# Causal mask of a recurrent-memory attention: from mask matmuls to an add on VectorE, with the subtraction of the maximum on GpSimd

## The chip, the cores and the metric

The kernel runs on one core of one Trainium2 chip. The metric is the device time of one execution in microseconds; lower is better. The engines are called PE (TensorE; PEld is its weight load), DVE (VectorE), ACT (ScalarE), POOL (GpSimd) and SP (SyncE, which here issues DMAs).

## The reference

Attention over segments of 32 tokens with 8 memory tokens that are handed from segment to segment, then a feed-forward block. 2048 tokens give 64 segments, which must run one after the other.

```python
S, Dm, H, Dh, M, seg = 2048, 640, 32, 128, 8, 32
idx  = arange(M + seg)
mask = (idx[:, None] < M) | (idx[:, None] >= idx[None, :])
mem  = mem0
for s in range(64):
    h = concat([mem, layernorm(x)[s*32:(s+1)*32]])      # 40 rows
    q, k, v = h @ Wq, h @ Wk, h @ Wv                     # per head
    scores = where(mask, q @ k.T * Dh**-0.5, -1e9)       # 40 x 40 per head
    o = softmax(scores) @ v @ Wo
    mem, out_s = o[:8], o[8:]
h  = x + concat(out_s)
h2 = h + relu(layernorm(h) @ w1 + b1)**2 @ w2 + b2
```

The memory rows of a segment see all 40 keys, the token rows only the keys up to their own.

## The kernel before, in words

The order of the instructions on every engine is the order in which the program issues them (a manual schedule); each engine works through its own list and waits where its data isn't there. One call of `step(b, sp)` handles one segment; 64 of them follow each other, with `b` the block of 128 tokens and `sp` the segment in it. A `tail` of 8 tokens of each segment is projected ahead of time for four segments at once, as work that needs no memory; such work lies in lists (`fill`, `late`, `mid`, `win`), from which `run` takes pieces at fixed places of a step.

Within a step, in this order on PE:

1. `project` (L392) multiplies the 32 rows of the segment (24 tokens and 8 memory rows, `hT4`) with Wq and Wk in halves of 16 heads. ACT takes the result out of PSUM into `row` (L222, L224, L405), DVE transposes it into `qT` and `kT` (L227, L408), POOL spreads the memory queries into `qz` (L374, L376).
2. `scores(n)` (L413) and `soft1`, `soft2` are the scores and the softmax of the memory rows, for `n` = 0 and 1.
3. `token_scores(n)` (L486) are the scores of the tokens of all 32 heads, in one PSUM bank `sk` seen as `skv` [128, 8, 40]: four groups of 32 partitions by eight heads by 40 keys. For `n` = 0 four mask matmuls (L489) stand ahead: the identity times `mask` puts 0 or -1e9 into the columns of the 32 token keys, and the score matmuls (L493) add to that in PSUM.
4. Between these lie the Wv projection (`proj` with `half`, evacuated by ACT in L502 and L523), `token_values` of the step before (L355, L360), and `values(n)` (L449, L454), whose results go to `oT` by DVE (L213) or ACT (L215).
5. DVE takes the maximum of `skv` over the keys (L527, `mxk`) and writes `tk` = `skv` - `mxk` to SBUF (L529).
6. `wo_rounds` (L238) is the output projection of the step's main rows into `pw`, with pieces of `fill` between.
7. ACT takes the exponential of `tk` (L542, `ek`); DVE sums it (L544, `zk`) and inverts the sum (L546, `rk`); POOL multiplies (L548 `pkt`, L551 `pk`).
8. `wo_out` (L241): ACT copies half of `pw` (L245, `otmp`, in the same buffer as `tk`), DVE adds the other half (L246, `o`). `mem_to_hT` (L312) transposes the eight new memory rows on PE (L316, `pm`) and DVE copies them into the next segment's `hT4` (L318). This is the recurrence: the next step's projections can't start before.
9. DVE transposes `pkt` and `pk` (L569 `pTt`, L575 `pTk`) for the `token_values` of the next step.

On ACT the order around the change is L523, L215, L542, L245; on DVE L440, L527, L529, L544, L546, L246, L318, L569, L575; on POOL L374 and L376, then L548, L551, L367 and the copies of the tails (L323, L325).

Of the kernel before, what the change touches and what calls it, by code (L numbers as in the profile page):

```python
# [9 lines left out]
ALU = mybir.AluOpType  # L10
AX = mybir.AxisListType
F32 = mybir.dt.float32
BF16 = mybir.dt.bfloat16
# [3 lines left out]
def kernel(  # L17
# [16 lines left out]
    nc = tc.nc  # L34
    _, S, D = A_x.shape
    _, H, E = A_Wq.shape
    M = A_mem0.shape[1]
    SEG = 32
    G = 4
    HG = H // G  # L40
# [8 lines left out]
    NK = SEG + M  # L49
# [6 lines left out]
    NEG = -1.0e9  # L56
# [4 lines left out]
    const = ctx.enter_context(tc.tile_pool(name="const", bufs=1))  # L61
# [6 lines left out]
    s1 = ctx.enter_context(tc.tile_pool(name="s1", bufs=1))  # L68
# [9 lines left out]
    ident = const.tile([128, 128], BF16)  # L78
# [3 lines left out]
    make_identity(nc, ident[:])  # L82
    mhalf = const.tile([128, 1], F32)
    nc.vector.memset(mhalf[:], -0.5)
    mask = const.tile([128, HG, SEG], BF16)
    nc.vector.memset(mask[:], 0.0)
    nc.gpsimd.affine_select(out=mask[0:32], in_=mask[0:32], compare_op=ALU.is_ge, fill=NEG, base=0,
                            pattern=[[0, HG], [-1, SEG]], channel_multiplier=1)
    bmask = const.tile([128, 4, TL], BF16)
    qz = const.tile([128, H, 32], BF16)  # L90
    nc.vector.memset(qz[:], 0.0)
# [10 lines left out]
    kT = const.tile([128, H, 2 * SEG], BF16)  # L102
# [33 lines left out]
    for ch in range(2):  # L136
        nc.scalar.dma_start(out=o0[32 * ch:32 * ch + M, :].rearrange("m (c f) -> m c f", f=64),
                            in_=A_mem0[0].rearrange("m (c t f) -> t m c f", t=2, f=64)[ch])
# [110 lines left out]
    fill, late, mid, win = [], [], [], []  # L249
# [130 lines left out]
    def step(b, sp, v=None):  # L380
# [53 lines left out]
        def soft2(n):  # L434
            rm = s2.tile([128, 1], F32, tag="rm", name="rm")
            nc.vector.reciprocal(out=rm[:], in_=zms[n][:])
            pm = s2.tile([128, 2 * SEG], BF16, tag="pmem", name="pmem")
            nc.vector.tensor_scalar(out=pm[:], in0=ems[n][:], scalar1=rm[:, 0:1], scalar2=None, op0=ALU.mult)
            pT = s2.tile([128, 2 * SEG], BF16, tag="pTm", name="pTm")
            nc.vector.transpose(out=pT[:], in_=pm[:])  # L440
            return pT
# [42 lines left out]
        skv = sk[:, 0:HG * NK].rearrange("p (i k) -> p i k", k=NK)  # L484

        def token_scores(n):  # L486
            if n == 0:
                for g in range(G):
                    nc.tensor.matmul(skv[32 * g:32 * g + 32, :, M:NK], lhsT=ident[:, 0:32], rhs=mask[:],  # L489
                                     start=True, stop=False, skip_group_check=True)  # L490
            for j in range(4):
                for g in range(G):
                    nc.tensor.matmul(skv[32 * g:32 * g + 32, n * 4 + j, :], lhsT=qT[:, n * 16 + g * 4 + j, M:NK],  # L493
                                     rhs=kT[:, n * 16 + g * 4 + j, 0:NK], start=False, stop=(n == 1 and j == 3),
                                     skip_group_check=True)

        token_scores(0)
        if ready:
            run(fill, DC)
# [8 lines left out]
        if not last:  # L508
            scores(1)
        token_scores(1)  # L510
        if not last:
            soft1(1)
# [10 lines left out]
            nc.scalar.copy(out=v[:, 512:1024], in_=ps1[:])  # L523
        if not last:
            pT1 = soft2(1)
        mxk = s1.tile([128, HG], F32, tag="mxk", name="mxk")
        nc.vector.tensor_reduce(out=mxk[:], in_=skv, op=ALU.max, axis=AX.X)  # L527
        tk = s1.tile([128, HG, NK], F32, tag="tk", name="tk")
        nc.vector.tensor_tensor(out=tk[:], in0=skv, in1=mxk[:].unsqueeze(2).to_broadcast([128, HG, NK]), op=ALU.subtract)  # L529

        pw = chn.tile([128, 512], F32, tag="ch", name="pw")
        main = lambda p: oT[:, p, 0:32]
# [1 line left out]
        if not last:  # L534
# [14 lines left out]
                                op=ALU.mult)  # L549
        pk = s1.tile([128, HG, 32], BF16, tag="pk", name="pk")  # L550
        nc.gpsimd.tensor_tensor(out=pk[:], in0=ek[:, :, 0:SEG], in1=rk[:].unsqueeze(2).to_broadcast([128, HG, SEG]),  # L551
                                op=ALU.mult)
# [18 lines left out]
        for u in range(2):  # L571
            nc.gpsimd.tensor_tensor(out=pTx[:, u], in0=pTt[:, u, HD:32].unsqueeze(1).to_broadcast([128, 4, TL]),
                                    in1=same[:], op=ALU.mult)
# [160 lines left out]
    for b in range(NB):  # L734
        for sp in range(4):
# [47 lines left out]
            if 2 <= e <= NK4 + 1:  # L783
                late.append(lambda e=e: prep_stats0(e - 2))
                mid.append(lambda e=e: prep_norm0(e - 2))
            step(b, sp, v0 if b + sp == 0 else None)

    def end_output(s):
# [18 lines left out]
    for t in range(S // NT):  # L807
# [6 lines left out]
        for fc in range(FC):  # L814
            ps = mmtile()
            for c in range(DC):
                if fc < FFULL:
                    nc.tensor.matmul(ps[:], lhsT=w1[:, c, fc * 128:(fc + 1) * 128], rhs=hnT[:, c, :],  # L818
                                     start=(c == 0), stop=(c == DC - 1))
                    continue  # L820
                for hh in range(2):
                    nc.tensor.matmul(ps[FREM * hh:FREM * (hh + 1), 0:HT], lhsT=w1[:, c, fc * 128:F],
                                     rhs=hnT[:, c, HT * hh:HT * (hh + 1)], start=(c == 0), stop=(c == DC - 1))
# [16 lines left out]
        for q in range(NK4):  # L840
# [6 lines left out]
            for hh in range(2):  # L847
                k = pr + 2 * hh
                for fc in range(FFULL):
                    nc.tensor.matmul(y[:, hh, 0:DH], lhsT=f1T[:, fc, k * 128:(k + 1) * 128], rhs=w2[:, fc, cs],  # L850
                                     start=(fc == 0), stop=False, skip_group_check=True)
# [3 lines left out]
            for hh in range(2):  # L855
                r = slice(FREM * hh, FREM * (hh + 1))
                nc.tensor.matmul(y[:, hh, 0:DH], lhsT=f1T[r, FFULL, pr * 128:(pr + 1) * 128], rhs=w2[r, FFULL, cs],
                                 start=False, stop=True, skip_group_check=True)
# [40 lines left out]
```

## Time and profile before

| | |
|---|---|
| median of 3 runs | 1029.64 us (1028.8 to 1029.67) |
| span of the profiled execution | 1025.5 us |
| the profiled execution's own time | not listed apart; span and median differ by 4.1 us |
| granted PE clock, mean | 0.997 |
| PE busy | 971.4 us (95%) |
| DVE, ACT, POOL busy | 619.0, 533.2, 309.1 us |
| mask matmuls L489 | 256, 273 ns each, 18.4 us |
| score matmuls L493 | 2048, 182 ns each, 36.7 us |
| DVE maximum L527, subtraction L529 | 64 each, 453 and 492 ns |
| ACT exponential L542 | 64, 473 ns |
| POOL products L548, L551 | 64 each, 294 and 615 ns |

Busy times overlap: four matmuls on 32 columns each run side by side, so the durations of the PE groups don't add up to the time that they hold PE. "Idle before" an instruction is the time in which its engine had nothing to do, with what ended it.

### The profile page before, as it was taken

To read this page: it belongs to the slowest core of one execution; us is meant where nothing else is said; L and a number is where in the kernel's file an instruction comes from. 1 tells how busy PE (TensorE), PEld (TensorE's weight loads), DVE (VectorE), ACT (ScalarE), POOL (GpSimd) and SP (SyncE) were. 2 spreads that over 40 slices of the span, in tenths; PEclk is the share of its full clock that TensorE was granted. 3 is DMA by queue.
4 is the path that set the end of the run, shared out by engine and by line. 5 is a ranking of instruction groups with operands and counts; after the bars stand their busy time and mean duration, and the time that the engine had idled before them with its cause. 6 is when DMAs were issued, how large, how long until landed. Compare 5 with 4: busy or idle time off the path is not lost.

```text
span 1025.5 us, 58960 instructions
## 1 busy us (share of the span) xinstructions
PE 971.4 (95%) x26951; PEld 576.6 (56%) x26960; DVE 619.0 (60%) x1740; ACT 533.2 (52%) x1229; POOL 309.1 (30%) x803
## 2 busy tenths in 40 slices
PE   5789999999999999999999999999999999999998
PEld 2345555655655555555655665555566565555565
DVE  2246666766666757666666666666666676466432
ACT  3335554555555555555555555555555555533431
POOL 1123333333333333333333332323232333443210
PEclk9989999999999999999999999999999999999999
DMA  9950101000101010001000000000000110612200
GB/s 367 397 180 21 23 7 30 7 25 6 35 7 31 6 40 8 26 11 31 11 25 11 26 16 20 17 15 27 14 22 8 47 34 7 204 55 65 77 26 26
DMA packets 39112, 51.57 MB, mean 50 GB/s; under 512 B 5968, under 2 KB 35024, under 8 KB 36944
## 3 DMA queue, kind: packets, MB, share of 16 engines
q1 hardware_dynamic: 38080, 47.48, 13.9%
q8 instruction: 210, 3.44, 1.4%
q10 hardware_dynamic: 784, 0.34, 0.1%
q14 instruction: 38, 0.31, 0.1%
HBM read 38.37 MB, written 9.44 MB: 47 GB/s over the span
## 4 chain that ended last, share of the span: by engine, by line
PE 87%; DMA 6%; DVE 2%; issue 2%; ACT 1%; SPq 1%; ACTq 0%; DVEq 0%; POOL 0%; POOLq 0%
PE ps L206 48%; PE pw L238 15%; PE y L850 5%; PE ps L818 4%; PE ps L238 3%; PE po L449 2%; PE po L355 2%; PE sm L421 2%; DMA wq<-in_B_w_dram 1%; DMA vt_d<-row 1%; PE ps L493 1%; DMA wv<-in_A_Wv_dram 1%; DMA wo<-in_A_Wo_dram 1%; PE pm L316 1%; DMA vt<-vt_d 1%
## 5 line engine op out<-in xcount | busy, mean ns | idle before, releaser
L206 PEld LDWEIGHTS <-hT 128*32 128x32 bf16 x7680 | 195.4, 97 | 179.6 <-issue 17.9
L238 PE MATMUL pw<-wo,oT 128*32 128x320 bf16 x4224 | 185.6, 300 | 7.6 <-issue 5.6
L206 PE MATMUL ps<-wv,hT 128*32 128x512 bf16 x2520 | 171.5, 379 | 2.3 <-issue 1.6
L206 PE MATMUL ps<-wq,hT 128*32 128x512 bf16 x2520 | 160.0, 382 | 5.3 <-DVE hT L318 5.3
L206 PE MATMUL ps<-wk,hT 128*32 128x512 bf16 x2520 | 159.3, 381 | 0.1
L238 PEld LDWEIGHTS <-oT 128*32 128x32 bf16 x4224 | 106.7, 96 | 59.8 <-issue 13.0
L222 ACT ACTIVATE row<-ps 128x512 bf16<-128x512 f32 x156 | 93.3, 599 | 75.5 <-PE ps L206 75.5
L227 DVE STREAM_TRANSPOSE qT<-row 128x512 bf16<-128x512 bf16 x128 | 90.3, 705 | 66.0 <-ACT row L222 65.9
L548 POOL TENSOR_TENSOR pkt<-ek,rk 128x64 bf16<-128x64 bf16 x64 | 18.8, 294 | 360.6 <-DVE rk L546 360.6
L224 ACT CAST row<-ps 128x512 bf16<-128x512 f32 x115 | 67.9, 591 | 33.1 <-PE ps L206 31.4
L325 POOL COPY kT<-kTt 128x1024 bf16<-128x1024 bf16 (+1 forms) x65 | 71.8, 1105 | 11.7 <-DVE kTt L227 11.7
L374 POOL COPY qz<-qT 128x96 bf16<-128x96 bf16 x126 | 33.4, 265 | 139.1 <-DVE qT L227 138.9
L206 PEld LDWEIGHTS <-hTt 128*32 128x32 bf16 x1920 | 53.6, 97 | 31.5 <-issue 1.3
L245 ACT COPY otmp<-pw 64x320 f32<-64x320 f32 x66 | 27.9, 422 | 81.3 <-PE pw L238 81.3
L365 ACT CAST oT<-po 128x512 bf16<-128x512 f32 x128 | 68.7, 589 | 1.6
L246 DVE TENSOR_TENSOR o<-pw,otmp 64x320 bf16<-64x320 f32 x66 | 31.8, 482 | 61.3 <-ACT otmp L245 61.3
L523 ACT CAST v<-ps 128x512 bf16<-128x512 f32 x63 | 36.9, 585 | 59.0 <-PE ps L206 59.0
L227 DVE STREAM_TRANSPOSE kT<-row 128x512 bf16<-128x512 bf16 x65 | 46.1, 709 | 31.1 <-ACT row L224 31.1
L544 DVE TENSOR_REDUCE zk<-ek 128x8 f32<-128x320 bf16 x64 | 31.1, 486 | 51.1 <-ACT ek L542 51.1
L850 PE MATMUL y<-wq,wk 128*128 128x320 bf16 x416 | 61.2, 299 | 0.4 <-DVE wk L827 0.4
L405 ACT CAST row<-ps 128x256 bf16<-128x256 f32 x126 | 40.7, 375 | 30.5 <-PE ps L206 29.9
L502 ACT CAST v<-ps 128x512 bf16<-128x512 f32 x63 | 36.9, 585 | 30.5 <-PE ps L206 30.5
(113 smaller groups left out, 1629.5 us busy)
## 6 DMA issues: line engine op xcount, KB each, us to landing
wv<-in_A_Wv_dram SPq DMA_DIRECT2D x5, 1024.0 KB
wq<-in_A_Wq_dram SPq DMA_DIRECT2D x5, 1024.0 KB
wk<-in_A_Wk_dram SPq DMA_DIRECT2D x5, 1024.0 KB
vt<-vt_d SPq DMA_DIRECT2D x60, 64.0 KB
xt<-in_A_x_dram SPq DMA_DIRECT2D x20, 160.0 KB
vt_d<-row SPq DMA_DIRECT2D x22, 128.0 KB
wo<-in_A_Wo_dram SPq DMA_DIRECT2D x2, 1280.0 KB
wo<-in_A_Wo_dram SPq DMA_DIRECT2D x4, 640.0 KB
```

The lines of the kernel that those rows point to most:

```text
L206: nc.tensor.matmul(ps[32 * k:32 * k + 32, :], lhsT=lhs(c), rhs=wr[:, c, n, k], start=(c == 0), stop=(c == DC - 1))
L222: nc.scalar.mul(out=row, in_=ps, mul=scale)
L224: nc.scalar.copy(out=row, in_=ps)
L227: nc.vector.transpose(out=dst[:, n * 16:(n + 1) * 16, 0:32], in_=row.rearrange("p (h e) -> p h e", e=32))
L238: nc.tensor.matmul(pw[32 * j:32 * j + 32, 0:DH], lhsT=lhs(p), rhs=wov2[:, head(p), ch], start=(h == 0), stop=(h == 15))
L325: nc.gpsimd.tensor_copy(out=kT[:, h0:h1, SEG:2 * SEG].rearrange("p h (j k) -> p h j k", k=TL), in_=k.unsqueeze(2).to_broadcast([128, h1 - ...
L365: nc.scalar.copy(out=oTg[:, n, :, :, M:NK], in_=po[:, :, n * 128:(n + 1) * 128].rearrange("p g (j q) -> p g j q", q=32))
L405: nc.scalar.copy(out=row[:, u * 256:(u + 1) * 256], in_=ps[:, u * 256:(u + 1) * 256])
L502: nc.scalar.copy(out=v[:, 0:512], in_=ps0[:])
L523: nc.scalar.copy(out=v[:, 512:1024], in_=ps1[:])
L818: nc.tensor.matmul(ps[:], lhsT=w1[:, c, fc * 128:(fc + 1) * 128], rhs=hnT[:, c, :], start=(c == 0), stop=(c == DC - 1))
L850: nc.tensor.matmul(y[:, hh, 0:DH], lhsT=f1T[:, fc, k * 128:(k + 1) * 128], rhs=w2[:, fc, cs], start=(fc == 0), stop=False, skip_group_chec ...
```

## The change

The mask becomes a tile of [128, 40] with all 40 keys, zero in the memory columns, and is copied to the other three groups of 32 partitions at the start. The mask matmuls go; the first score matmul of each partition group starts the accumulation. DVE adds the mask while it takes the scores out of PSUM into `tk`, takes the maximum from `tk` in SBUF, and POOL subtracts the maximum from `tk` in place. The exponential then waits for POOL instead of DVE.

```diff
-    mask = const.tile([128, HG, SEG], BF16)
+    mask = const.tile([128, NK], BF16)
     nc.vector.memset(mask[:], 0.0)
-    nc.gpsimd.affine_select(out=mask[0:32], in_=mask[0:32], compare_op=ALU.is_ge, fill=NEG, base=0,
-                            pattern=[[0, HG], [-1, SEG]], channel_multiplier=1)
+    nc.gpsimd.affine_select(out=mask[0:32, M:NK], in_=mask[0:32, M:NK], compare_op=ALU.is_ge, fill=NEG, base=0,
+                            pattern=[[-1, SEG]], channel_multiplier=1)
+    for g in range(1, G):
+        nc.vector.tensor_copy(out=mask[32 * g:32 * g + 32], in_=mask[0:32])
...
         def token_scores(n):
-            if n == 0:
-                for g in range(G):
-                    nc.tensor.matmul(skv[32 * g:32 * g + 32, :, M:NK], lhsT=ident[:, 0:32], rhs=mask[:],
-                                     start=True, stop=False, skip_group_check=True)
             for j in range(4):
                 for g in range(G):
                     nc.tensor.matmul(skv[32 * g:32 * g + 32, n * 4 + j, :], lhsT=qT[:, n * 16 + g * 4 + j, M:NK],
-                                     rhs=kT[:, n * 16 + g * 4 + j, 0:NK], start=False, stop=(n == 1 and j == 3),
+                                     rhs=kT[:, n * 16 + g * 4 + j, 0:NK], start=(n == 0 and j == 0), stop=(n == 1 and j == 3),
                                      skip_group_check=True)
...
+        tk = s1.tile([128, HG, NK], F32, tag="tk", name="tk")
+        nc.vector.tensor_tensor(out=tk[:], in0=skv, in1=mask[:].unsqueeze(1).to_broadcast([128, HG, NK]), op=ALU.add)
         mxk = s1.tile([128, HG], F32, tag="mxk", name="mxk")
-        nc.vector.tensor_reduce(out=mxk[:], in_=skv, op=ALU.max, axis=AX.X)
-        tk = s1.tile([128, HG, NK], F32, tag="tk", name="tk")
-        nc.vector.tensor_tensor(out=tk[:], in0=skv, in1=mxk[:].unsqueeze(2).to_broadcast([128, HG, NK]), op=ALU.subtract)
+        nc.vector.tensor_reduce(out=mxk[:], in_=tk[:], op=ALU.max, axis=AX.X)
+        nc.gpsimd.tensor_tensor(out=tk[:], in0=tk[:], in1=mxk[:].unsqueeze(2).to_broadcast([128, HG, NK]), op=ALU.subtract)
```

## The prediction, made before the changed kernel was run

> **What bounds the kernel now.** I read the page first (busy time, then the chain that ended last), then the groups of instructions by line, the chain in order of time for four steps, and the timeline of one step.
>
> From the page, busy time and the chain:
>
> ```profile
> PE 971.4 (95%) x26951; PEld 576.6 (56%) x26960; DVE 619.0 (60%) x1740; ACT 533.2 (52%) x1229; POOL 309.1 (30%) x803
> ...
> PE 87%; DMA 6%; DVE 2%; issue 2%; ACT 1%; SPq 1%; ACTq 0%; DVEq 0%; POOL 0%; POOLq 0%
> ```
>
> TensorE carries the end; what it no longer does is gained unless something makes it wait. The chain in order of time says what the mask costs there and where waits of others enter:
>
> ```profile
> 534.11 4.50 PE ps L206 x80
> ...
> 539.19 0.11 PE ps L489 x4
> ...
> 546.11 0.11 PE pm L316 x19
> ```
>
> ```profile
> 532.49 0.43 ACT otmp L245
> ...
> 532.95 0.49 DVE o L246
> ...
> 533.48 0.35 PE pm L316 x20
> ...
> 533.86 0.21 DVE hT L318
> ```
>
> The four mask matmuls hold TensorE for about 0.11 us. The second excerpt is the recurrence: `otmp` (ACT), `o` (DVE), `pm` (PE), `hT` (DVE), then the next step's projections. It stands on the chain in the steps in which TensorE has too little other work there. The timeline of one step shows how tight the rest is:
>
> ```profile
> 333.14 0.45 DVE L527 TENSOR_REDUCE mxk<-ps 128x8 f32<-128x320 f32 x1
> 333.63 0.49 DVE L529 TENSOR_TENSOR tk<-ps,mxk 128x320 f32<-128x320 f32 x1
> ...
> 334.22 0.47 ACT L542 ACTIVATE ek<-tk 128x320 bf16<-128x320 f32 x1
> ...
> 334.73 0.49 DVE L544 TENSOR_REDUCE zk<-ek 128x8 f32<-128x320 bf16 x1 [0.61 <-ACT ek L542]
> 335.25 0.20 DVE L546 RECIPROCAL rk<-zk 128x8 f32<-128x8 f32 x1
> ...
> 335.60 0.30 POOL L548 TENSOR_TENSOR pkt<-ek,rk 128x64 bf16<-128x64 bf16 x1 [5.31 <-DVE rk L546]
> 335.78 0.42 ACT L245 COPY otmp<-pw 64x320 f32<-64x320 f32 x1 [1.08 <-PE pw L238]
> 335.85 0.61 POOL L551 TENSOR_TENSOR pk<-ek,rk 128x256 bf16<-128x256 bf16 x1
> ...
> 336.24 0.48 DVE L246 TENSOR_TENSOR o<-pw,otmp 64x320 bf16<-64x320 f32 x1 [0.78 <-ACT otmp L245]
> ...
> 336.77 0.21 PEld L316 LDWEIGHTS <-o 128*32 128x32 bf16 x20 [0.30 <-DVE o L246]
> ```
>
> Read: `ek` starts 0.10 after `tk` ends. Behind `ek`, ACT idles 1.08 until the output projection `pw` is done. DVE idles 0.78 between `rk` and `o`; that is the cover for a later `ek`, because `zk` and `rk` stand ahead of `o` in DVE's order. And the weight load of `pm` already waits for `o` (0.30): a late `o` stops TensorE.
>
> **The change part by part.**
>
> *Removed from TensorE:* 4 mask matmuls and 4 weight loads in each of 64 steps. The matmul group says 273 ns each, but four run side by side in the four column groups; on the chain all L489 pieces sum to 6.8 us (62 pieces, 0.11 each). Before the next wait of TensorE for DVE or POOL there is slack: in the step at 513 us `scores(1)` starts 0.4 us after `kT` is complete. So **-6.8 us**. The first score matmul now waits for the PSUM buffer in the mask's place; that wait ends early (0.2 us once in the whole run).
>
> *DVE:* the order is add, maximum instead of maximum, subtract. The add reads the same 128x320 f32 PSUM scores as L529 and writes the same tile: 0.49. The maximum now reads SBUF; `zk` (L544), a reduction of as many elements from SBUF, takes 0.486 against 0.453 for L527: +0.03. The PSUM scores are read once, so the bank is free earlier; no wait for it shows, so nothing is gained.
>
> *The subtraction on POOL* (128x320 f32). POOL is free: 5.3 us of idle before `pkt`, and the new instruction stands directly ahead of `pkt` in its order; behind it wait `pkt`, `pk` and, through `ek`, everything of this softmax. Cost from POOL's rows: two-input bf16 rows give 240 ns for 32 elements, 294 for 64, 615 for 256, so 187 + 1.67 ns an element, 0.72 us for 320. The only wide f32 row, L648 (f32 out of bf16, 640 elements, 1493 ns), gives 2.04 ns an element over the same 187, so 0.84. With f32 inputs as well I take **0.86**; bounds 0.70 and, f32 inputs being nowhere in the rows, 1.2.
>
> The Trainium skill, GPSIMD Engine Reference, section 4.1, speaks against the change: elementwise work belongs on VectorE, GpSimd being about twice as slow with two inputs. No row here shows a POOL operation with f32 inputs of this width; what the rule would give is rival 3.
>
> *Hand-over.* DVE to POOL takes 0.15 (`rk` ends 335.45, `pkt` starts 335.60); POOL to ACT isn't seen; I take ACT's 0.10 behind DVE, which was there before (bounds 0.03, POOL to DVE, and 0.15). So `ek` comes later by 0.03 + 0.15 + 0.86 = **1.04 us** after the moment when its data was ready.
>
> *What of that reaches TensorE.* ACT: `ek` would end 1.04 later in a gap of 1.08, just inside. DVE: `zk` and `rk` move with `ek`, and `o` comes late by 1.04 minus the gap between `rk` and `o`. Independent DVE instructions start up to 0.08 before the one ahead ends (`pTt` and `pTk`), dependent ones 0.04 after; I give 0.05 of overlap. The timelines of all 63 steps that hand a memory on fall into these classes:
> - 8 steps like the one shown, gap 0.79: 1.04 - 0.84 = 0.20 each, 1.6 us.
> - 14 steps in which `ek` already waits 0.04 to 0.3 (0.1 on average) for ACT's copy L215 ahead of it: about 0.12 each, 1.65 us.
> - 13 steps in which that wait is over 0.3 (0.69 on average): nothing.
> - 14 steps with gaps of 0.94 to 1.6, where TensorE itself was late: 0.05 us in all.
> - 14 steps in which TensorE still has output-projection matmuls of the tails (L238) queued ahead of `pm`; there `pm` starts 0.24 after `o`, so 0.17 to spare: 0.1 us in all.
>
> Together **+3.4 us**. It reaches the end in full in the first two classes: `pm` waits for `o`, `hT` for `pm`, and the next projection for `hT`. The waits list has 47 weight loads of L316 behind `o` and 49 of L206 behind `hT`.
>
> *Nothing else on the path.* `pkt` and `pk` end about 1 us later. `pk` would end 0.6 us after `o`, while `pTk` (L575) starts 0.7 after `o` in the tightest step that I looked at (508.08 against 507.34); if that 0.1 of cover went, the next step's transposes on DVE, which idle 0.4 first, would still be in time. POOL's L367 waited 0.90 for ACT after `pk`, so `oTt` and the tail copies behind it move by some 0.1; TensorE waits for POOL only twice in the whole run (1.7 and 0.6 us). If that cover went, the scores of the next step would be late by those 0.1. Start: three 32x40 copies (0.15 each by L97) on DVE, beside weight loads that the chain shows until 59 us: nothing.
>
> **Sum.** -6.8 + 3.4 = -3.4 us on the span of 1025.5 us. The profiled execution's time isn't listed apart; the median, 1029.64, lies 4.1 above the span, launch and end, which the change doesn't touch. Forecast **1026.2 us**. 0.2% (2.06 us) is about what can be told from no change.
>
> **Rivals.**
> 1. *POOL's pass is hidden whole* (0.72 us, or the stalls before `pm` are mostly TensorE's own): by the classes 0.6 us reach TensorE; -6.2, 1023.4, and 1022.8 at best. For: the bf16 rows; the chain passes through `o` in only 13 steps. Against: f32, and the weight load's 0.30 behind `o`. Chance 0.14.
> 2. *Slower: the POOL pass is dearer and `o` becomes the bound in most steps.* The point is 0.96 us: there the classes sum to 6.4, just under the saving; at 1.1 they give 12.0, so +5.2 (1034.8); at 1.2, 16.6 and +9.8 (1039.4). The same holds for longer hand-overs: what counts is `ek` 1.14 late. Past it the gap on ACT (1.08) is used up too. For: the gaps are alike in most steps, so each further 0.1 costs 4 us, and nothing in the trace shows f32 inputs on POOL. Against: it needs 15% more than the f32 row extrapolates to. Chance 0.23.
> 3. *A gain of nothing: POOL takes twice VectorE's time.* Twice L529's 0.49 is 0.98; by the classes 7.1 us come back, +0.3, 1029.9. For: where the rows allow a comparison, POOL is slower by more than that (640 elements: L648 1493 ns, f32 out, against DVE's L638 484, all bf16). Against: L648 itself, scaled to 320, is 1.7 times L529. Chance 0.09. This is the rule of section 4.1 named above.
> 4. *The mask's time isn't TensorE's.* 28 stalls of 0.2 us and more on the chain, 12.5 us, are "issue", in stretches of many short instructions; the mask matmuls are four long ones ahead of such a stretch and may give it time. If the stalls take back some 3 us of the 6.8, the result is 1029.6. Against: also 512 instructions fewer to bring in. Chance 0.11.
>
> My forecast, from -5.8 to -1.3: 0.43.
>
> **How the numbers follow.** Faster by over 0.2%: 0.36 of the forecast's 0.43 (the rest of it lies above -2.06), and rival 1's 0.14, together 0.50. Slower: 0.22 of rival 2, 0.04 of rival 3, which sits near the line, and 0.02 of rival 4, together 0.28. Same: the rest, 0.22. The range starts 1.3 below rival 1's best, for stalls that fall otherwise (1021.5), and reaches into rival 2 to a pass of 1.09 us (1034.0); beyond both lie 2 in 10. The forecast's own range is 1023.8 to 1028.3.
>
> **What would show it.** In the profile after: no mask matmuls, and score matmuls directly behind the projections; a POOL group of 64 at 0.8 to 0.9 us; `ek` at 1.0 to 1.1 later behind the DVE start of its chain; the idle time of DVE before `o`, 71.2 us now, down to about 20, and TensorE's loads waiting for `o` in more steps and longer than 21.1 us. Wrong if POOL takes over 0.96, if `otmp` waits for `ek`, or if "issue" grows by more than 2 us.

## The result and the profile after

| | before | after |
|---|---|---|
| median beside the prediction (4 runs each) | 1029.66 us | 1023.81 us (1020.68 to 1024.77) |
| ratio, 95% interval | | 0.9937 (0.9918 to 0.9956) |
| second and third comparison (5 rounds each) | 1030.06, 1026.45 us | 1022.06, 1018.61 us |
| their ratios | | 0.9928 (0.9902 to 0.9953), 0.9920 (0.9901 to 0.9938) |
| span of the first profiled execution | 1025.5 us | 1018.6 us (run time 1020.68) |

The change makes the kernel 0.6 to 0.8% faster, 6 to 8 us. The forecast was 1026.2 in a range of 1021.5 to 1034.0: the sign was right, but the 3.4 us that it had put down for a late `o` did not come, and the time came out where rival 1, given a chance of 0.14, put it (all of GpSimd's pass hidden). The later comparisons lie lower still: their ratios applied to 1029.64 give 1022.2 and 1021.4 us, the second just under the range.

The page after, busy time and chain by engine:

```profile
PE 962.5 (94%) x26695; PEld 566.2 (56%) x26704; DVE 617.6 (61%) x1743; ACT 538.9 (53%) x1229; POOL 354.2 (35%) x867
...
PE 87%; DMA 6%; DVE 3%; issue 2%; ACT 1%; SPq 0%; POOL 0%; DVEq 0%; ACTq 0%; POOLq 0%
```

256 matmuls fewer on PE, 64 instructions and 45 us more on POOL, and POOL still 0% of the chain: the new pass hardly stands on the chain that ended last. What it costs, the experiments say. The groups of instructions that answer to L527 and L529 of before (busy, mean ns of one, idle time before it and its releaser):

```profile
L528 POOL TENSOR_TENSOR tk<-tk,mxk 128x320 f32<-128x320 f32 x64 | 46.2, 722 | 253.6 <-DVE mxk L527 245.0 <-ACT oT L217 4.8 <-ACT v L521 3.8
...
L527 DVE TENSOR_REDUCE mxk<-tk 128x8 f32<-128x320 f32 x64 | 31.1, 486 | 2.2
...
L541 ACT ACTIVATE ek<-tk 128x320 bf16<-128x320 f32 x64 | 30.1, 470 | 29.9 <-POOL tk L528 29.5
...
L525 DVE TENSOR_TENSOR tk<-ps,mask 128x320 f32<-128x320 f32 x64 | 29.0, 453 | 0.8 <-PE ps L491 0.8
```

The subtraction takes 0.722 us, not the 0.86 that I had put in. The timeline of one step, with little to spare, from the add to the next memory:

```profile
800.07 0.45 DVE L525 TENSOR_TENSOR tk<-ps,mask 128x320 f32<-128x320 f32 x1
800.56 0.49 DVE L527 TENSOR_REDUCE mxk<-tk 128x8 f32<-128x320 f32 x1
...
801.19 0.72 POOL L528 TENSOR_TENSOR tk<-tk,mxk 128x320 f32<-128x320 f32 x1 [3.79 <-DVE mxk L527]
...
801.95 0.47 ACT L541 ACTIVATE ek<-tk 128x320 bf16<-128x320 f32 x1 [0.69 <-POOL tk L528]
802.45 0.49 DVE L543 TENSOR_REDUCE zk<-ek 128x8 f32<-128x320 bf16 x1 [1.40 <-ACT ek L541]
802.71 0.42 ACT L247 COPY otmp<-pw 64x320 f32<-64x320 f32 x1 [0.29 <-PE pw L240]
802.97 0.20 DVE L545 RECIPROCAL rk<-zk 128x8 f32<-128x8 f32 x1
...
803.17 0.48 DVE L248 TENSOR_TENSOR o<-pw,otmp 64x320 bf16<-64x320 f32 x1
...
803.70 0.21 PEld L318 LDWEIGHTS <-o 128*32 128x32 bf16 x20 [0.30 <-DVE o L248]
```

From the start of the add to `ek` it is 1.88 us; before it was 1.08. `rk` ends at 803.17 and `o` starts at 803.17, still 0.04 after `otmp` (803.13), as before. So the lateness of `ek` has eaten DVE's gap to the last tenth, and `o` isn't late. ACT idles 0.29 where it idled 1.08. The weight load waits 0.30 for `o`, the same as in the step shown of before.

The waits of the whole run say the same (us in total, times, longest), before and after:

```profile
DVE o L246 <- ACT otmp L245: 71.2, 78, 3.2
...
PEld L316 <- DVE o L246: 21.1, 47, 1.4
```

```profile
DVE o L248 <- ACT otmp L247: 32.7, 53, 3.0
...
PEld L318 <- DVE o L248: 21.2, 47, 1.4
```

VectorE's wait ahead of `o` is used up by more than half, and TensorE's wait for `o` has not grown. From the last matmul of `pw` to the start of `o` it is 35.7 us in sum over the 64 steps before, and 35.9 after.

I use one more reading below: the loop, from the copy of the new memory (`hT`) in step 1 to that in step 62. It took 799.2 us before and 792.8, 794.4 and 791.0 us in three profiles after, 0.08 to 0.13 us less a step. The profiled loop leaves out the start and the feed-forward block.

### The profile page after: what moved, and what is told of

Same layout as the page of the kernel before. It is cut to its first block, busy times and chain, and to the rows that moved or that the text cites. A ratio compares the mean times of both kernels' runs of the same rounds, so it can differ in the third digit from the quotient of the medians.

```text
span 1018.6 us, 58497 instructions
## 1 busy us (share of the span) xinstructions
PE 962.5 (94%) x26695; PEld 566.2 (56%) x26704; DVE 617.6 (61%) x1743; ACT 538.9 (53%) x1229; POOL 354.2 (35%) x867
## 4 chain that ended last, share of the span: by engine, by line
PE 87%; DMA 6%; DVE 3%; issue 2%; ACT 1%; SPq 0%; POOL 0%; DVEq 0%; ACTq 0%; POOLq 0%
PE ps L208 48%; PE pw L240 15%; PE y L849 5%; PE ps L817 4%; PE ps L240 3%; DMA wk<-in_A_Wk_dram 3%; PE po L451 2%; PE po L357 2%; PE sm L423 2%; DMA wq<-in_B_w_dram 2%; DMA xt<-in_A_x_dram 1%; PE ps L491 1%; PE pm L318 1%; DVE o L248 1%; DVE wk L826 1%
## 5 line engine op out<-in xcount | busy, mean ns | idle before, releaser
L208 PEld LDWEIGHTS <-hT 128*32 128x32 bf16 x7680 | 193.3, 97 | 179.4 <-issue 15.5
L208 PE MATMUL ps<-wv,hT 128*32 128x512 bf16 x2520 | 166.2, 380 | 1.9 <-issue 1.2
L528 POOL TENSOR_TENSOR tk<-tk,mxk 128x320 f32<-128x320 f32 x64 | 46.2, 722 | 253.6 <-DVE mxk L527 245.0
L521 ACT CAST v<-ps 128x512 bf16<-128x512 f32 x63 | 36.9, 585 | 56.0 <-PE ps L208 56.0
L849 PE MATMUL y<-wq,wk 128*128 128x320 bf16 x416 | 61.2, 300 | 0.4 <-DVE wk L826 0.2
L825 ACT ACTIVATE wv<-ps,b1f 128x512 bf16<-128x512 f32 (+1 forms) x56 | 37.6, 672 | 28.2 <-PE ps L817 27.8
L432 ACT ACTIVATE em<-sm,mx 128x64 bf16<-128x64 f32 x126 | 40.4, 321 | 20.9 <-DVE mx L429 20.8
```

Source lines behind the costliest of these rows:

```text
L208: nc.tensor.matmul(ps[32 * k:32 * k + 32, :], lhsT=lhs(c), rhs=wr[:, c, n, k], start=(c == 0), stop=(c == DC - 1))
L432: nc.scalar.activation(out=em[:], in_=sms[n][:, 0:2 * SEG], func=ACT.Exp, bias=mx[:, 0:1], scale=1.0, accum_out=zm[:])
L528: nc.gpsimd.tensor_tensor(out=tk[:], in0=tk[:], in1=mxk[:].unsqueeze(2).to_broadcast([128, HG, NK]), op=ALU.subtract)
```

## The experiments

Theory A: TensorE no longer holds its time for the mask, and the later exponential is hidden. The experiments ran in four sets. The kernel before ran beside each of them, the changed kernel beside the first and the last; where variants of two sets are compared, it is by their ratios to the kernel before in their own set.

**The changed kernel again**, twice (results in the table above).

> The changed kernel again, beside the experiments. Theory A (TensorE no longer holds 0.107 us a step for the mask, and the later exponential is hidden): 5 to 7 us under before, about 1023.5. Rival B (the gain comes from reading the score bank once and from a lighter VectorE): the same figure; the other runs tell them apart.

> The changed kernel beside the last variant. Theory A: 0.991 to 0.995 of the kernel before, as in the two comparisons so far.

By the ratios 7.4 and 8.2 us under the kernel before, at the upper end of what was expected or just over it. Single runs of the same kernel differ by 3 to 9 us, so differences under some 2 us are not resolved by medians here.

**Both masks.** Is it the mask matmuls, or the lighter VectorE and the score bank that is read once?

```diff
         def token_scores(n):
+            if n == 0:
+                for g in range(G):
+                    nc.tensor.matmul(skv[32*g:32*g+32, :, M:NK], lhsT=ident[:, 0:32], rhs=maskp[:], start=True, stop=False, ...)
...
-   ... start=(n == 0 and j == 0), ...
+   ... start=False, ...
```

> The changed kernel with the four mask matmuls put back as well, so that the mask is added twice; VectorE and GpSimd work as in the changed kernel. Theory A: the whole gain goes, 0 to 1 us from before (1029.7). Rival B: the gain stays, about 1024. In between, say 1027, would mean that each carries a part.

Measured: 1030.77 us, ratio 1.0008 (0.9994 to 1.0022). The groups show the changed kernel's subtraction and the old matmuls side by side:

```profile
L536 POOL TENSOR_TENSOR tk<-tk,mxk 128x320 f32<-128x320 f32 x64 | 46.2, 722 | 260.8 <-DVE mxk L535 260.8
...
L495 PE MATMUL ps<-maskp,ident 128*32 128x256 bf16 x256 | 18.3, 273 | 0.2 <-ACT row L411 0.2
```

The whole gain is gone, and nothing is lost beyond it: rival B falls, and the move to GpSimd by itself costs nothing that can be measured (the interval allows up to 0.2%). From 1.0008 to 0.9928, in the same set, it is 8 us for the four matmuls.

**The mask twice on PE** (the kernel before with eight mask matmuls a step):

```diff
                 for g in range(G):
                     nc.tensor.matmul(skv[...], lhsT=ident[:, 0:32], rhs=mask[:], start=True, stop=False, ...)
+                for g in range(G):
+                    nc.tensor.matmul(skv[...], lhsT=ident[:, 0:32], rhs=mask[:], start=False, stop=False, ...)
```

> The kernel before with eight mask matmuls a step instead of four (the mask is added twice). Theory A: 0.107 us a step more, 6.8 us slower than before, about 1036.5. Rival E (short waits of TensorE absorb part of it): 3 us or less.

Measured: 1035.6 against 1027.04 us, ratio 1.0079 (1.0058 to 1.0100), +8.1 us (6.0 to 10.3). Divided by 64 steps, four mask matmuls cost 0.13 us (0.09 to 0.16); the chain's pieces had said 0.107, which is inside. No wait of TensorE absorbs them.

**The subtraction on VectorE.**

```diff
-        nc.gpsimd.tensor_tensor(out=tk[:], in0=tk[:], in1=mxk..., op=ALU.subtract)
+        nc.vector.tensor_tensor(out=tk[:], in0=tk[:], in1=mxk..., op=ALU.subtract)
```

> The changed kernel with the subtraction on VectorE instead of GpSimd, so the exponential comes about 0.5 us later than in the kernel before instead of 0.75. Theory A: both are inside the cover (0.79 us between the reciprocal and the sum for o), so the same as the changed kernel within 1 us. Rival C (the GpSimd pass, which ends just as the cover does, costs part of the gain): 1 to 2 us faster than the changed kernel.

Measured: 1021.12 us, ratio 0.9922 (0.9901 to 0.9944), against 0.9928 for the changed kernel beside it. The same, within what can be told. The pass takes 492 ns there against 722 on GpSimd, and none of the difference is seen at the end.

```profile
L528 DVE TENSOR_TENSOR tk<-tk,mxk 128x320 f32<-128x320 f32 x64 | 31.5, 492 | 2.2
```

**No maximum.**

```diff
-        nc.vector.tensor_reduce(out=mxk[:], in_=tk[:], op=ALU.max, axis=AX.X)
-        nc.gpsimd.tensor_tensor(out=tk[:], in0=tk[:], in1=mxk..., op=ALU.subtract)
```

> The changed kernel without the maximum and its subtraction (left out: the stabilisation of the token softmax). The exponential comes 0.5 us earlier than in the kernel before. Theory A (everything ahead of the exponential is hidden already): within 1 us of the changed kernel. Rival C (the GpSimd pass costs part of the gain): 1 to 3 us faster than the changed kernel.

Measured: 1018.45 us, ratio 0.9913 (0.9891 to 0.9934); loop 792.6 us, between the changed kernel's three. The data of the exponential is ready some 1.3 us earlier than in the changed kernel. `ek` itself starts no earlier than in the kernel before, though 0.5 us was expected: it now stands directly behind ACT's own copy L217.

```profile
L538 ACT ACTIVATE ek<-tk 128x320 bf16<-128x320 f32 x64 | 30.3, 473 | 0.1
```

The ratios differ by 1.5 us, which is within the scatter (their sets are not the same). What stands ahead of the exponential is hidden already, as far as this can be told.

**GpSimd longer by a copy of 8 elements.** This puts `ek` where the prediction had expected it.

```diff
...
+        nc.gpsimd.tensor_copy(out=mxc[:], in_=mxk[:])
-        nc.gpsimd.tensor_tensor(out=tk[:], in0=tk[:], in1=mxk..., op=ALU.subtract)
+        nc.gpsimd.tensor_tensor(out=tk[:], in0=tk[:], in1=mxc..., op=ALU.subtract)
```

> A copy of the 8 maxima stands ahead of the subtraction on GpSimd, so the exponential comes 0.2 to 0.3 us later still, about 1.05 us later than in the kernel before: the lateness that the prediction had counted on. Theory A with the classes of the prediction (cover 0.79 plus 0.08 of overlap in most steps): 3 to 4 us slower than the changed kernel, about 1027. Rival D (TensorE does not really wait for o in most steps, so the cover is larger than the gap on VectorE): within 1 us of the changed kernel.

Measured: 1023.62 us, ratio 0.9933 (0.9912 to 0.9954); the changed kernel beside it 1022.06, 0.9928. The timeline of a step:

```profile
659.83 0.45 DVE L525 TENSOR_TENSOR tk<-ps,mask 128x320 f32<-128x320 f32 x1
...
660.93 0.19 POOL L529 COPY mxc<-mxk 128x8 f32<-128x8 f32 x1 [3.84 <-DVE mxk L527]
...
661.20 0.72 POOL L530 TENSOR_TENSOR tk<-tk,mxc 128x320 f32<-128x320 f32 x1
661.96 0.47 ACT L543 ACTIVATE ek<-tk 128x320 bf16<-128x320 f32 x1 [0.94 <-POOL tk L530]
...
662.47 0.42 ACT L247 COPY otmp<-pw 64x320 f32<-64x320 f32 x1
...
662.98 0.20 DVE L547 RECIPROCAL rk<-zk 128x8 f32<-128x8 f32 x1
663.10 0.47 DVE L248 TENSOR_TENSOR o<-pw,otmp 64x320 bf16<-64x320 f32 x1
```

`ek` starts 2.13 us after the add, 1.05 later than before, and the cover is gone: `o` starts 0.21 after `otmp` ends instead of 0.04, and 0.08 ahead of `rk`'s end, about the earliest of any step in these runs (0.09). That lateness adds up to 3.9 us in 29 steps, and the waits list has 24.7 us of weight loads behind `o` against 21.2. The lateness of `o` is the predicted one in the predicted size. The time does not show it: 1.6 us in the medians and 0.5 by the ratios, under the 3 to 4 that were expected and not told apart from rival D's 1 us. The next two answer with a bigger dose.

**Two passes on GpSimd**, once with a second full operand and once with the subtraction done twice.

```diff
+        nc.gpsimd.tensor_tensor(out=tk[:], in0=tk[:], in1=tk[:], op=ALU.add)      # first variant
         nc.gpsimd.tensor_tensor(out=tk[:], in0=tk[:], in1=mxk..., op=ALU.subtract)
+        nc.gpsimd.tensor_tensor(out=tk[:], in0=tk[:], in1=mxk..., op=ALU.subtract) # second variant
```

> The changed kernel with one more GpSimd pass ahead of the subtraction, which adds the score tile to itself (this doubles the scores, so the softmax is of other values; the work is otherwise the same). Its second operand is the full f32 tile and not a repeated value. Price of that pass: 0.72 us if GpSimd goes by 1.67 ns an element whatever the operands; 0.84 or more if a full second operand costs more, as the wide f32 row of the kernel before (2.04 ns an element) suggests. Theory A: the exponential comes 1.55 to 1.75 us later than in the kernel before, and by the classes of the prediction (cover 0.79 plus 0.08) 23 to 35 us come on top of the changed kernel. Rival D (TensorE does not wait for o in most steps, so the cover is larger than VectorE's gap): under 12 us.

> The changed kernel with the subtraction done twice on GpSimd (the softmax is the same for any shift); both passes have the repeated operand, 0.72 us each. The exponential comes 1.5 to 1.6 us later than in the kernel before. Theory A by the classes: 21 to 27 us slower than the changed kernel, 1044 to 1050. Rival D: under 12 us, 1035 at most.

Measured: 1045.13 us, ratio 1.0123 (1.0108 to 1.0138), and 1044.38 us, ratio 1.0105 (1.0068 to 1.0142). The groups of the first:

```profile
L529 POOL TENSOR_TENSOR tk<-tk,mxk 128x320 f32<-128x320 f32 x64 | 46.2, 723 | 5.0
...
L528 POOL TENSOR_TENSOR tk<-tk 128x320 f32<-128x320 f32 x64 | 46.0, 719 | 254.8 <-DVE mxk L527 254.8
```

The price is 0.72 us with either kind of second operand. Of the second, the waits list (us in total, times, longest) and the chain from 600 to 604 us:

```profile
PEld L318 <- DVE o L248: 45.1, 61, 2.2
...
PE pm L318 <- DVE o L248: 21.2, 36, 1.8
```

```profile
599.82 0.73 POOL tk L528
...
600.62 0.73 POOL tk L529
...
601.38 0.48 ACT ek L542
...
601.88 0.50 DVE zk L544
...
602.52 0.48 DVE o L248
```

Now the softmax of the tokens stands on the chain, and TensorE's matmuls wait 21.2 us for `o` instead of 6.6. `ek` is 1.59 us later than before, and in 53 and 52 of the 64 steps ACT goes from `ek` to `otmp` within 0.15 us: the gap on ACT is used up too, as rival 2 had it. From the last matmul of `pw` to the start of `o` it is 61.8 and 61.2 us in sum, against 35.9 in the changed kernel: `o` is 25 to 26 us late.

By the classes that gives 25 us over the changed kernel. The ratios give less: 0.0123 and 0.0105 over the kernel before, and 0.0072 from there to the changed kernel, 18 to 20 us. Both lie below what was expected (23 to 35 and 21 to 27). Rival D (under 12) falls; the measured cost is a fifth to a quarter below the classes. The profiled loops, 816.7 and 818.0 us against 791.0 to 794.4, say 22 to 27, but they come from different sets: the kernel before took 1032.12 us beside these two, and 1029.66, 1030.06 and 1026.45 beside the three profiles of the changed kernel. Less these differences 20 to 23 us are left, and the second's profiled execution was 2.4 us over its median.

**The other mask moved too**, and that with the subtraction on VectorE:

```diff
         def scores(n):
...
-            for g in range(G):
-                nc.tensor.matmul(sm[32*g:32*g+32, SEG:2*SEG], lhsT=ident[:, 0:32], rhs=bmask..., start=True, ...)
...
-                ... start=False, ...
+                ... start=(j == 0), ...
...
         def soft1(n):
+            nc.vector.tensor_tensor(out=sms[n][:, SEG:2*SEG], in0=sms[n][:, SEG:2*SEG], in1=bmask..., op=ALU.add)
```

> The changed kernel with the other mask moved as well: the four 32-column mask matmuls ahead of the memory scores (two sets a step) go, and VectorE adds that mask in PSUM ahead of the maximum (two more instructions of about 0.2 us a step). Theory A: TensorE holds each set for about 0.02 us, so 2.5 us at most, 1020.5, if the 0.2 us in the memory softmax stay inside its slack of 0.3 to 0.5 us. Rival: the slack is used up (VectorE transposes kT behind that maximum), and it comes out 3 us or more slower than the changed kernel.

> Both masks added by VectorE and the subtraction on VectorE too, so GpSimd has no new work and the exponential of the token scores comes 0.5 us earlier than in the changed kernel. Theory A: the memory mask's matmuls give about 2 us more than the changed kernel (1021.5 if that has 1023.5), and the earlier exponential gives back what a late o costs where VectorE now has two more instructions a step (0.3 us in all). Rival C (VectorE, with three instructions more a step, becomes late for the memory softmax): no gain over the changed kernel, or a loss of 1 to 3 us.

Measured: 0.9930 (0.9906 to 0.9953) for the first, 1019.48 us, and 0.9950 (0.9931 to 0.9969) for the second, 1022.28 us, where the changed kernel beside it had 0.9920. Neither beats the changed kernel; the second is likely slower by 0.3%, though its `ek` comes 0.3 us earlier than in the changed kernel (0.5 was expected). In the first, VectorE's idle time ahead of the memory scores is 3.2 us in the whole run (ahead of the add). It was 17.3 ahead of the maximum in the kernel before, but only 10.4 to 10.8 in the changed kernel already. So VectorE mostly comes to these scores late by itself. First the changed kernel, then this one:

```profile
L429 DVE TENSOR_REDUCE mx<-sm 128x1 f32<-128x64 f32 x126 | 28.0, 222 | 10.4 <-PE sm L423 2.3
```

```profile
L428 DVE TENSOR_REDUCE mx<-sm 128x1 f32<-128x64 f32 x126 | 28.3, 224 | 4.3
...
L426 DVE TENSOR_TENSOR sm<-sm,bmask 128x32 f32<-128x32 f32 x126 | 23.4, 186 | 3.2 <-PE sm L420 3.2
```

The 32-column matmuls had held TensorE for only 0.02 us a set on the chain (2.0 us in all), and 23.4 us of VectorE are paid for them; that this is why nothing is gained is argued, not shown. The loop of the first was 790.8 us, at the low end of the changed kernel's three; that of the second 792.6. What makes the second slower isn't settled: its chain shows 17.5 us of "issue" stalls over 0.2 us each in the loop, the most of all variants, against 12.7 to 14.9 in three profiles of the changed kernel.

## Why the prediction was right, and which term was off

- *The mask matmuls, -6.8 us: right, and rather low.* Putting them back costs 8 us, doubling them 8.1 (6.0 to 10.3).
- *DVE's part, +0.03: it is nil.* The add takes 453 ns, not the 492 of the old subtraction, and the maximum from SBUF 486, not 453: the two durations have changed places.
- *POOL's pass, 0.86: this is the term that was mis-sized.* It takes 0.722, and 187 + 1.67 ns an element, fitted on the bf16 rows, gives 0.721. I had moved away from it for the one wide row with f32, L648, which makes f32 out of bf16. The all-f32 tile of 320 elements takes what the line through the bf16 rows gives. The bounds held it (0.70 to 1.2), the value taken didn't.
- *The hand-overs, 0.15 and 0.10: the second was too dear as well.* DVE to POOL was 0.08 to 0.17, POOL to ACT 0.03 to 0.04. With the pass this makes `ek` 0.73 to 0.82 later, not 1.04.
- *The classes, +3.4: they gave nothing, because 0.82 lies inside 0.79 plus 0.08 of overlap.* For the lateness of `o` the classes stand: at 1.05 its sum was 3.9 us against 3 to 4 expected, and at 1.59 it is 25 to 26 against 25. That this reaches the end in full is not shown: at 1.05 the ratios have 0.5 us, which isn't resolved, and at 1.59 they have 18 to 20.
- *The range held partly by luck.* It had been drawn to take in rival 1, and rival 1 is what happened; the mechanism that gave the forecast its own figure, a late `o`, did not appear.
- *Rival 1 came true* (a pass of 0.72, all hidden; 1022.8 to 1023.4 forecast, 1023.81 measured). *Rival 2's mechanism is real*, and two passes show it; by the numbers above the single pass ends short of it by 0.05 to 0.14 us. *Rival 3* falls with the price: 722 against 492 is 1.5 times VectorE, and the Trainium skill's rule (GPSIMD Engine Reference, section 4.1: about twice as slow, elementwise work on VectorE) would have left a gain of nothing; the measurement decides against it here, on the price and on the gain. *Rival 4* (issue stalls take the gain back): the chain's issue stalls over 0.2 us rose from 12.0 us in the loop to 14.6, 14.9 and 12.7 in three profiles after, but they are 16.1 with both masks and 13.1 with the mask twice. They scatter with the code and from run to run, and don't follow the mask.
- Of the signs named ahead: no mask matmuls, yes; POOL at 0.8 to 0.9, no, 0.72; DVE's idle time before `o` down from 71.2 to 20, it went to 32.7; loads behind `o` above 21.1, no, 21.2, which is the plainest sign that all is hidden. Of the signs of being wrong, GpSimd over 0.96 did not come, and `otmp` stands directly behind `ek` in one of the 64 steps. "Issue" up by more than 2 us did come, in two of the three profiles (2.6 and 2.9), and the gain was there all the same.

## What to carry to other kernels

On a kernel that TensorE carries, work taken off it is gained in full only if what replaces it ends inside a gap that another wait has already opened: measure that gap on the engine whose order it stands in (here VectorE, `rk` to `o`), and not the share of busy time. Price an operation that the trace doesn't show by the row with the same kind of inputs and outputs, and don't correct it by a row that converts types. A move that ends just inside its cover is free and also at its end: 0.25 us more and the wait shows in the trace, 0.8 more and the kernel is 18 to 20 us slower than with the single pass.

## What the runs showed of the hardware that I had not expected

- GpSimd's two-input pass costs, with f32 at 320 elements, what the bf16 rows of 32 to 256 give (1.67 ns an element over 187 ns: 0.721 us against 0.722 measured), and the same with a full second operand as with a repeated one (719 and 723 ns). The conversion row L648, f32 out of bf16, costs 2.04 ns an element.
- A hand-over depends on the pair of engines, not on the receiver alone: VectorE to ACT 0.10 us, VectorE to GpSimd 0.08 to 0.17, but GpSimd to ACT 0.03 to 0.04.
- Adding a bf16 mask in SBUF to f32 scores in PSUM took 453 ns where subtracting an f32 maximum took 492 (from PSUM and from SBUF alike), over the same 128x320. The two differ in the type of the second operand and in how it is repeated; which of these counts is not shown.
